# A new list of steps for a sliding-window attention and expert-attention kernel: first unit loaded in row halves, weights in halves, whole-array turns, last stores in four

## The chip, the cores and the metric

The kernel runs on one core of one Trainium2 chip. The metric is the device time of one execution in microseconds (us), as the median of several runs. Its engines are named as in the profile: PE does matmuls (PEld its weight loads), DVE is the vector engine, ACT the scalar engine, POOL the general one, SP the one that issues most loads and stores.

## The reference

Two stages follow each other. The first is attention with a symmetric window of 32 positions, for 8 batches, 8 heads, 576 positions and 64 values per head. The second takes its result as x (576 x 512 per batch) through four attention experts, of which each position uses the two with the largest gate.

```python
# stage 1, q, k, v: (8, 8, 576, 64)
scores = q @ k.T / 8
scores = where(abs(i - j) <= 32, scores, -1e9)
x = softmax(scores) @ v            # -> (8, 576, 512)
# stage 2
logits = x @ w_gate                # 4 experts
w = softmax over the 2 largest logits
for e in range(4):                 # causal attention, width 64
    q, k, v = x @ wq[e], x @ wk[e], x @ wv[e]
    ye = softmax(causal(q @ k.T / 8)) @ v @ wo[e]
    out += (weight of e at each position) * ye
```

## The kernel before, in words

The whole program is one hand-written list, `ORDER`: some 900 short step names, each a function call with its batch and part, the engine behind a colon (v = DVE, a = ACT, g = POOL) and the PSUM banks behind an @. Every engine runs its own steps in the list's order, and waits by semaphores for the data that it needs. A load (`load`, L183) also waits for the last PE instruction that stands before it in the list, so its place in the list sets when SP issues it. Stores wait only for their data, in SP's order.

The steps of one batch b, in the order of the data:

- `lq`, `lk` load four heads of q or k (a unit g = 0 or 1, 0.59 MB); `lv` loads a fifth of v (128 rows of all heads, 256 KB; the last 64 rows, 128 KB). The first two units of batch 0 are loaded in two parts each, of two-row pieces, with four DMAs to a part, some on ACT's queue (form t); all others in one DMA of 18 rows per partition (form e). NAT holds three units of q and three of k.
- `tq`, `tk` turn a unit on DVE (L292 for whole units, L296 for the pieces). `vc` copies v's halves side by side.
- `sc` computes a half of a unit's scores in float32 (80 matmuls), `ex` takes exponentials on ACT (L337), `mk` multiplies by the window's mask on POOL (L341).
- `av` multiplies with v for one of five row groups (32 matmuls), `un` divides by the sums on DVE, `xt`/`xf`/`xb` turn the result and copy it to float32 and bfloat16.
- `ga`, `gt`, `ge`, `gm`, `gu` compute the gate. `pp`/`pe` project q and k for a pair of experts, `pv`/`ve` v.
- `ps`/`xe`/`se` compute causal scores, exponentials (ACT) and the causal cut (POOL), `po`/`oe` the products with v, weighted by the gate.
- `pt`/`ot` turn these (five turns of up to 128 columns), `py` multiplies by wo, `ye` copies the result to one of three Y buffers (one for each w = 0, 1, 2), `st` stores it. w = 0 and 1 are 256 rows each (512 KB), w = 2 the last 64 rows.

The weights wq, wk and wv are loaded whole in `lw0`, `lw1`, `lw2`, through the Y buffers, and cast by `cw0`, `cw1`, `cw2`; wo by `lw3` and `cw3`. Batches overlap: while stage 2 of one batch runs, stage 1 of the next ones does.

## Time and profile before

| what | value |
|---|---|
| median of 3 runs | 270.59 us (270.17 to 270.87) |
| profiled execution | 272.21 us, span 270.5 us |
| PE busy | 224.7 us, 83% of the span |
| DVE, POOL, ACT busy | 172.4, 156.1, 153.1 us |
| DMA moved | 40.66 MB, mean 150 GB/s |

The span goes from the first to the last instruction of the profiled execution. In an order of time, the bracket behind a row is the idle time of the engine just before it, and what ended that; "issue" stands where the profile shows nothing that the engine waited for.

### The profile page before, as it was taken

The numbers are of one execution on the slowest core, as the hardware profiler recorded it, in microseconds if no ns is written. First come the engines' busy times: TensorE is split into PE (matmuls) and PEld (weight loads), VectorE is DVE, ScalarE is ACT, GpSimd is POOL, SyncE is SP. The second block draws the span as 40 slices with busy tenths as digits, with TensorE's granted clock in tenths as the row PEclk, the third lists the DMA queues.
The fourth block names the chain that finished last, engine by engine and source line by source line (L and its number), as shares of the span: only waits on it lengthen the run. The fifth ranks groups of instructions, "written<-read, shape, count | busy, mean of one in ns | idle before, by whom it ended". The sixth has DMA issues, their size and how long they took to land.

```text
span 270.5 us, 12380 instructions
## 1 busy us (share of the span) xinstructions
PE 224.7 (83%) x5526; PEld 180.3 (67%) x5536; DVE 172.4 (64%) x353; ACT 153.1 (57%) x241; POOL 156.1 (58%) x192
## 2 busy tenths in 40 slices
PE   0464468998996999988796999969999899999980
PEld 0443457877886887857675688857787768866640
DVE  0658533865872898577687168568856668675770
ACT  0232233885573696666662469627787655776721
POOL 5048742998596659647968816258929883211400
PEclk9999997999997999999999799979999999999996
DMA  7899693695699697426488243602230042202565
GB/s 159 197 273 243 104 257 99 140 295 182 133 269 237 151 288 213 141 58 159 130 238 288 47 99 74 154 2 95 97 110 12 6 155 82 99 21 80 182 244 198
DMA packets 59350, 40.66 MB, mean 150 GB/s; under 512 B 45728, under 2 KB 51360, under 8 KB 59296
## 3 DMA queue, kind: packets, MB, share of 16 engines
q1 hardware_dynamic: 56736, 38.68, 52.1%
q10 hardware_dynamic: 2560, 1.18, 1.9%
q8 instruction: 43, 0.70, 1.1%
q14 instruction: 11, 0.09, 0.1%
HBM read 30.42 MB, written 9.44 MB: 147 GB/s over the span
## 4 chain that ended last, share of the span: by engine, by line
PE 72%; DMA 11%; issue 8%; DVE 4%; ACT 3%; ACTq 0%; SPq 0%; DVEq 0%
PE PS L177 63%; PE PS L180 9%; DMA qn<-in_q_dram 4%; DMA out_dram<-Y 3%; DMA kn<-in_k_dram 2%; DMA V<-in_v_dram 1%; ACT A L337 1%; DVE Tkn L292 1%; DVE Tqn L292 1%; ACT Y L169 1%; DVE Y L171 0%; ACT VE L169 0%; ACTq L183 0%; ACT WV L169 0%; ACT WK L169 0%
## 5 line engine op out<-in xcount | busy, mean ns | idle before, releaser
L341 POOL TENSOR_TENSOR A<-A,MASKP 128x576 f32<-128x576 f32 x64 | 89.5, 1413 | 37.5 <-ACT A L337 36.9
L177 PE MATMUL PS<-Tqn,Tkn 32*64 32x128 f32 (+3 forms) x2560 | 52.5, 297 | 28.7 <-issue 11.2
L177 PEld LDWEIGHTS PS<-Tqn,Tkn 32*64 32x64 f32 x2560 | 44.9, 148 | 35.7 <-issue 19.1
L337 ACT ACTIVATE A<-PS 128x576 f32<-128x576 f32 x64 | 38.6, 651 | 44.9 <-PE PS L177 44.8
L516 POOL TENSOR_SCALAR_AFFINE_SELECT ATE<-ATE 128x256 bf16<-128x256 bf16 (+1 forms) x80 | 28.9, 383 | 43.1 <-ACT ATE L511 33.5
L511 ACT ACTIVATE ATE<-PS 128x1024 bf16<-128x1024 f32 x48 | 47.6, 1026 | 9.6 <-PE PS L177 9.3
L177 PE MATMUL PS<-V,A 128*64 128x65 f32 (+1 forms) x1280 | 42.1, 227 | 5.2 <-issue 5.1
L177 PEld LDWEIGHTS PS<-V,A 128*64 128x64 f32 (+1 forms) x1280 | 38.1, 136 | 9.2 <-issue 6.7
L292 DVE STREAM_TRANSPOSE Tkn<-kn 128x576 f32<-128x576 f32 x28 | 32.6, 1243 | 5.1 <-PE PS L177 3.2
L292 DVE STREAM_TRANSPOSE Tqn<-qn 128x576 f32<-128x576 f32 x28 | 32.2, 1242 | 3.0 <-PE PS L177 1.9
L171 POOL CAST XTB<-XTF 128x1024 bf16<-128x1024 f32 (+1 forms) x18 | 12.5, 706 | 18.5 <-DVE XTF L171 6.9
L369 DVE TENSOR_TENSOR XN<-PS,RC 128x512 f32<-128x512 f32 x32 | 22.1, 692 | 1.3 <-DVE RC L368 0.2
L169 ACT COPY XTF<-PS 128x128 f32<-128x128 f32 (+1 forms) x23 | 13.4, 632 | 16.4 <-PE PS L180 13.3
L368 DVE RECIPROCAL RC<-PS 128x8 f32<-128x8 f32 x32 | 6.5, 205 | 22.8 <-PE PS L177 22.4
L180 PE MATMUL PS<-ident,XN 128*128 128x128 f32 x144 | 20.9, 294 | 0.0
L171 POOL COPY V<-V 64x2048 f32<-64x2048 f32 (+1 forms) x12 | 20.6, 1717 | 0.4
L169 ACT CAST QKE<-PS 128x576 bf16<-128x576 f32 x23 | 14.4, 642 | 9.3 <-PE PS L177 9.1
L177 PE MATMUL PS<-VE,ATE 128*128 128x65 bf16 x480 | 17.5, 193 | 2.7 <-issue 1.5
L177 PE MATMUL PS<-XTB,WQ 128*128 128x288 bf16 x128 | 19.6, 302 | 0.0
L171 DVE COPY Y<-PS 128x1024 f32<-128x1024 f32 (+1 forms) x12 | 11.5, 956 | 12.7 <-PE PS L177 10.5
L177 PEld LDWEIGHTS <-ATE 128*128 128x128 bf16 x480 | 16.2, 97 | 4.9 <-issue 4.0
L177 PE MATMUL PS<-WO,OTT 128*128 128x512 bf16 (+1 forms) x86 | 18.4, 344 | 1.0 <-DVE OTT L171 0.3
(70 smaller groups left out, 285.0 us busy)
## 6 DMA issues: line engine op xcount, KB each, us to landing
V<-in_v_dram SPq DMA_DIRECT2D x32, 256.0 KB, 4.0
out_dram<-Y SPq DMA_DIRECT2D x16, 512.0 KB, 3.3
kn<-in_k_dram SPq DMA_DIRECT2D x14, 576.0 KB, 5.5
qn<-in_q_dram SPq DMA_DIRECT2D x14, 576.0 KB, 5.4
V<-in_v_dram SPq DMA_DIRECT2D x8, 128.0 KB, 4.3
out_dram<-Y SPq DMA_DIRECT2D x16, 64.0 KB, 2.8
Y<-in_moe_wq_dram SPq DMA_DIRECT2D x1, 512.0 KB, 7.5
Y<-in_moe_wk_dram SPq DMA_DIRECT2D x1, 512.0 KB, 4.0
```

The lines of the kernel that those rows point to most:

```text
L169: nc.scalar.copy(o, i)
L171: eng(c).tensor_copy(o, i)
L177: last_pe[0] = nc.tensor.matmul(*a, **kw)
L180: last_pe[0] = nc.tensor.transpose(*a)
L292: nc.vector.transpose(T[:, :].rearrange("q (p o) -> q o p", o=18)[:, o0:o1], n_[:, o0:o1, 32 * dh:32 * dh + 32])
L337: nc.scalar.activation(AT[(2 * b + g) % NAT_][half][p], two(b0)[:, :, 0:HS], EXP, scale=scale_att)
L341: eng(c).tensor_tensor(out=ap, in0=ap, in1=MASK[:, None, HS * half:HS * half + HS].to_broadcast([128, 2, HS]), op=MULT)
L368: nc.vector.reciprocal(rc, u[:, :, :, 64])
L369: nc.vector.tensor_tensor(out=XN[T // 2][:, T % 2, :].rearrange("p (g h d) -> p g h d", g=2, h=4), in0=u[:, :, :, 0:64], in1=rc[:, :, :, N ...
L511: nc.scalar.activation(chunk(A, ch), two(b0), EXP, scale=scale_moe)
L516: nc.gpsimd.affine_select(ap, ap, pattern=[[0, n], [1, w]], compare_op=IS_GE, fill=0.0, base=0, channel_multiplier=-1)
```

## The change

`ORDER` is written anew as a whole: nearly every step has another place, often another engine for its copies and other banks. In the new list:

- The first unit (batch 0, g = 1; now ahead of g = 0) is loaded and turned in two halves of 9 rows per partition (288 KB in one DMA each); one of the four goes on ACT's queue (form f). g = 0 is loaded whole.
- wq and wk are loaded and cast in halves of two experts (`lw`, `cw` with two numbers), the gate's weights in a step of their own (`lwg`).
- Five steps `zz` are new: each has four matmuls of a zeroed tile, 128 x 128 by 128 x 512, into a bank that nobody reads. `s_zero` zeroes the tile.
- `pt` turns 128 columns in all five turns.
- For batch 7, w = 0 and 1 are computed, copied and stored in two halves each (`py`, `ye`, `st` with a third number): four stores of 256 KB instead of two of 512.

```diff
 ORDER = """
-    lk011:t lq002 s_ones lq011 lq001:t lk001 tq011:v tq002:v tk011:v tq001:v tk001:v lk012:t lv00 lk002 s_warm tk012:v
-    tk002:v s_pads lk100:e sc010@02 lq012:t lv03 lq100:e lv02 sc000@46 ex0000@4 ex0100@0 ex0101@2 s_mask lv01 sc001@40
-    lq110:e lk110:e tk100:e lv04 tq012:v ex0001@6 lw0 sc011@26 ex0010@4 ex0011@0 tq100:e sc100@04 lw1 lk200:e lw2
...
-    oe61@2 ps710@4 xe712@6 xe701@0 py51@6 st42 xe710@4 se713 se710 se701 se703 se700 py50@0 pt60@2 pt61@3 st40 ps711@4
-    ye51:a@6 ye50:v@0 xe711@4 po70@6 ot60:v@2 py52@2 ot61:v@3 ye52:v@2 py61@0 oe70@6 st51 se712 se711 po71@4 oe71@4
-    py60@2 py62@6 pt70@7 st50 pt71@4 ot70:v@7 ot71:v@4 ye61:a@0 ye60:a@2 st52 st61 st60 ye62:v@6 py71@0 ye71:v@0
-    py70@2 py72@4 st62 ye70:a@2 ye72:v@4 st71 st70 st72
+    lq011:f lq012:e lk011:e lk012:e s_warm tq011:e tq012:e tk011:e lq000:e s_ones lk000:e s_zero tk012:e tq000:e
+    lq100:e sc011@02 lk100:e lv03 tk000:e s_pads sc010@46 ex0111@2 lv01 lv00 ex0100@4 zz0@2 s_mask zz3@2 ex0101@6
+    sc000@24 s_ident ex0110@0 mk0111:g ex0001@4 lv02 lwg sc001@06 tq100:e tk100:e mk0101:g mk0110:g zz1@4 ex0011@6
+    ex0000@2 zz2@4 lk110:e lw10 lv12 lv04 mk0001:g mk0100:g mk0011:g ex0010@0 tk110:e vc00:a sc100@46 sc101@02 lq110:e
+    lw00 ex1000@4 vc01:g ex1001@6 mk0000:g av00@4 ex1010@0 un00@4 av01@6 lv11 mk0010:g av02@0 mk1001:g un01@6 un02@0
+    av03@4 ex1011@2 lw11 mk1011:g cw10:g av04@0 lk200:e un03@4 un04@0 lq200:e xt00@2 tq110:e xf00:a@2 xt02@0 xt01@4
+    sc111@62 xf02:a@0 mk1010:g xf01:a@4 xb01:g xb02:g lv10 tk200:e xb00:a cw00:a ex1110@6 sc110@04 ex1101@4 cw11:g
+    lv13 ex1111@2 pp000@6 pp001@4 lw01 pe000:a@6 mk1101:g mk1111:g mk1000:g pe001:v@4 ex1100@0 pp011@2 tq200:e lv14
+    ps001@6 lw2 xe001@6 ps002@0 ga0@4 xe002@0 sc200@60 pe011:a@2 lq210:e cw01:a pp010@2 gt0@4 ge0@4 vc11:g gm0@4
...
+    ps710@2 xe701@4 xe700@6 se711 se700 pt60@1 se713 ge7@0 se701 se712 xe710@2 se710 gm7@0 py50@4 pv70@6 ot60:a@1
+    ve70:a@6 gu7@0 py61@2 py62@0 ye62:a@0 ye61:a@2 ye50:v@4 po70@4 oe70@4 po71@6 oe71@6 py60@0 pt70@2 ot70:v@2 pt71@3
+    ot71:v@3 py72@2 st50 py710@3 st62 py711@4 st61 ye72:v@2 ye60:a@0 st60 ye710:a@3 st72 ye711:v@4 py701@2 st710 st711
+    py700@3 ye701:a@2 st701 ye700:a@3 st700
 """
...
+    ZERO = sb.tile([128, 512], BF16, name="ZERO")
...
+    def s_zero():
+        nc.vector.memset(ZERO, 0.0)
+
+    def zz(c, n, b0):
+        for _ in range(4):
+            mm(PS[:, b0, :], ZERO[:, 0:128], ZERO, start=True, stop=True)
...
-    def lw0():
+    def lwg():
         load(WG[:, :, 0:4], moe_w_gate.rearrange("(t p) e -> p t e", p=128))
-        load(WST[0].rearrange("p (e t d) -> p e t d", e=4, t=4), moe_wq.rearrange("e (t p) d -> p e t d", p=128))
...
+    def lw(n, j):
+        load(WST[n][:, 512 * j:512 * j + 512].rearrange("p (e t d) -> p e t d", e=2, t=4),
+             (moe_wq, moe_wk)[n][2 * j:2 * j + 2].rearrange("e (t p) d -> p e t d", p=128))
...
         for t in range(NQT):
-            w = 128 if t < 4 else 64
-            turn_pe(o[:, 128 * t:128 * t + w], O[0:w, t, :, :].rearrange("p e d -> p (e d)"), ident_bf[0:w, 0:w])
+            turn_pe(o[:, 128 * t:128 * t + 128], O[:, t, :, :].rearrange("p e d -> p (e d)"), ident_bf)
...
+        elif len(at) == 2:
+            copy(c, ysb(b, w)[:, at[0], :], one(at[1]))
...
+        elif at:
+            r = 256 * w + 128 * at[0]
+            nc.sync.dma_start(out[b, r:r + 128, :], ysb(b, w)[:, at[0], :])
```

## The prediction

> **What bounds the kernel now.** I read the page's first lines first, then the stretches, then TensorE's own order of time.

> ```profile
> span 270.5 us, 12380 instructions
> ...
> PE 224.7 (83%) x5526; PEld 180.3 (67%) x5536; DVE 172.4 (64%) x353; ACT 153.1 (57%) x241; POOL 156.1 (58%) x192
> ...
> q8 instruction: 43, 0.70, 1.1%
> ```

> PE is the bound: 224.7 us of 270.5, and no other engine is over 64%. The instruction queue q8 brought 0.70 MB in 43 packets, about 16 KB each. PE and PEld together have 11,062 instructions, which over 43 packets is 257 each: one packet is 128 matmuls with their weight loads.

> ```profile
> 0.00:10.40 10.40, 0.03 (x4) 0.03 (x4) 2.26 (x8) 1.43 (x2) 3.81 (x12) 1.00 0.74 175
> 10.40:47.00 36.60, 23.42 (x668) 20.48 (x676) 19.76 (x49) 11.06 (x16) 17.30 (x17) 0.95 0.83 196
> 47.00:150.00 103.00, 92.38 (x2675) 76.43 (x2674) 74.35 (x140) 66.95 (x111) 78.47 (x79) 0.98 0.71 192
> 150.00:252.60 102.60, 98.89 (x2080) 77.77 (x2086) 67.73 (x143) 67.74 (x109) 53.98 (x79) 0.97 0.26 77
> 252.60:270.50 17.90, 9.95 (x116) 5.58 (x117) 8.31 (x16) 5.96 (x7) 2.50 (x7) 0.85 0.61 219
> ```

> Columns: stretch, length, busy PE, PEld, DVE, ACT, POOL, granted clock, DMA share, GB/s. PE's 45.8 idle us are 10.4 before the first matmul, 13.2 by 47 us, 10.6 by 150, 3.7 by 252.6, and 8.0 in the tail. DMA is at 0.83 just where PE idles most; 175 GB/s x 10.4 us and 196 x 36.6 make 9.0 MB by 47 us.

> What stops PE between 10 and 47 us is in its order of time (bracket: idle time before, and what ended it):

> ```profile
> 10.38 4.33 PE L177 MATMUL PS<-Tqn,Tkn 32*64 32x96 f32 x160 [10.38 <-DVE Tkn L296]
> 15.88 2.40 PE L177 MATMUL PS<-Tqn,Tkn 32*64 32x64 f32 x63 [1.17 <-ACT A L337]
> 19.12 0.81 PE L177 MATMUL PS<-Tqn,Tkn 32*64 32x96 f32 x17 [0.84 <-issue]
> 23.64 3.33 PE L177 MATMUL PS<-Tqn,Tkn 32*64 32x64 f32 x110 [3.70 <-DVE Tqn L296]
> 30.42 3.24 PE L177 MATMUL PS<-Tqn,Tkn 32*64 32x160 f32 x128 [3.46 <-issue]
> 34.15 0.32 PE L177 MATMUL PS<-Tqn,Tkn 32*64 32x96 f32 x2 [0.49 <-issue]
> 34.40 3.95 PE L177 MATMUL PS<-V,A 128*64 128x65 f32 x124
> 41.75 1.39 PE L177 MATMUL PS<-V,A 128*32 128x65 f32 x36 [3.40 <-issue]
> ...
> 46.86 1.35 PE L177 MATMUL PS<-Tqn,Tkn 32*64 32x96 f32 x79
> ```

> Add the counts between stops marked "issue": 160+63 = 223, 17+110 = 127, 128, 2+124 = 126. PE halts every 128 matmuls, waiting for no engine: it waits for its next packet. So the time from one such place to the next is the larger of the 128 matmuls' work and a **turnaround**: 30.42-19.12 = 11.3 us, 34.15-30.42 = 3.7, 41.75-34.15 = 7.6. The queue that issues the loads says why they differ:

> ```profile
> 24.11 0.51 SPq L183 DMA_DIRECT2D Y<-in_moe_wq_dram  x1
> 32.06 0.37 SPq L183 DMA_DIRECT2D Y<-in_moe_wk_dram  x1
> 32.47 1.27 SPq L183 DMA_DIRECT2D kn<-in_k_dram  x1
> 33.79 0.43 SPq L183 DMA_DIRECT2D Y<-in_moe_wv_dram  x1
> 34.32 4.41 SPq L183 DMA_DIRECT2D qn<-in_q_dram  x1
> ```

> Nothing was issued from 24.6 to 32.06, and the turnaround from 30.42 was the shortest, 3.7; four loads were issued in the 2.3 us around 34.15, and it was 7.6. [...]

> **The change, part by part.** Estimates from rows, against this execution (272.21 us for its 270.5 span, 1.7 around it).

> *First unit in halves.* Before, the first scores need four-row pieces, many DMAs each; after, four 288 KB halves, issued at once on two queues.

> ```profile
> L341 POOL TENSOR_TENSOR A<-A,MASKP 128x576 f32<-128x576 f32 x64 | 89.5, 1413 | 37.5 <-ACT A L337 36.9
> ...
> L292 DVE STREAM_TRANSPOSE Tkn<-kn 128x576 f32<-128x576 f32 x28 | 32.6, 1243 | 5.1 <-PE PS L177 3.2
> ...
> V<-in_v_dram SPq DMA_DIRECT2D x32, 256.0 KB, 4.0
> ...
> kn<-in_k_dram SPq DMA_DIRECT2D x14, 576.0 KB, 5.5
> ```

> 288 KB lies between 4.0 and 5.5 us to landing. Issued at about 0.8, the first half is there at 4.8; then VectorE has eight half transposes, as much as four whole ones: 4 x 1.243 = 5.0 us, with two small memsets about 10.2. That is the old 10.38: no gain at the first matmul (9.8 to 12). But now both halves of this unit are there, where the old list ran out and waited 3.70 us at 23.64 for its second q half.

> From 10.2: two scores steps (160 matmuls, 4.33 us) to 14.5; meanwhile four whole transposes for the other unit, 5.0, to 15.2. The new zz steps (16 of the 20 dummy matmuls lie here) fill that gap: 8 x 0.21 = 1.7 us, from the 128x512 group below, to 16.3. The first packet is asked for at about the 96th matmul (224 less 128), at 12.8; before, the same place came at 12.6 (10.38 + 96 x 0.027) and PE went on at 19.12, so 19.3 here, with the queue as full. Scores sc000's rest and sc001 (2.8) and two more zz (1.7) bring 23.8; tq100/tk100 are done by 15.2 + about 2 of pad memsets + 5.0 = 22.3. The next place is just behind, 24.5 by a turnaround of 5.2 (3.7 to 7.6: 23.0 to 26.9). Then comes the one block that is all scores, 2.2 us of work (128/160 x 2 x 1.35); four loads are issued just ahead of it, turnaround 5 (3.7 to 7.6): 29.5. POOL's eight masks at 1.413 and a V copy behind the exponentials end at about 28 to 29, beside it. The old list had these 480 matmuls done at 34.40: -4.9. Then 160 av matmuls at 3.95/124, 5.1 us: 34.6; transposes to 37; lq110, listed after sc101, lands 5.5 after 29.5 and turns in 2.5: 37.5. The next scores start at 38.0 where they started at 46.86: **-8.9**. Ends: by then 8.4 MB must have come (units of 0.59 MB, V pieces of 0.26, weight halves of 0.26); at 196 GB/s that is 43, so -4; without any stop in the all-scores block, -11.

> *Weights in halves.* 0.26 MB pieces that stand in different blocks. But lw01, lv14 and lw2, 0.9 MB, stand in the last 1.3 us ahead of one place (behind sc110 and three pp's), with 3.9 us of work behind it: turnaround 6 to 7.6, and pp010 needs lw01 (4.0 us to landing and a cast): **+2.5** (0 to +5).

> *The later blocks.* I cut both lists into 128s and summed each block's work from 1.35 per scores step, 0.97 per av, 0.97 per pp, 1.0 per po and so on. The old list has four whole blocks of little but scores, 2.1 us each, at the places that stopped PE most; of the later stops these are the largest:

> ```profile
> 81.49 2.11 issue
> ...
> 145.51 2.49 issue
> ```

> All "issue" pieces of 0.4 us or more on the chain from 60 us on make 10.35 us. The new list has no block of 2.1 after the first units; its shortest are 3.05 and 3.2, the others 3.65 to 10. With 3.7 quiet, 4.5 to 5 where loads stand in the last 3 us ahead of the place (nine of them, among them sc500, sc510 and sc601), I get 1.0+0.5+0.3+0.8+0.4+1.8+0.6+0.5+0.6 = 6.5: **-3.9** (from -8 to +1; a load issued just ahead of a place may also come too late to disturb its packet).

> *zz and whole-array turns.* The fifth zz (zz4) lies in busy work: four matmuls of 128x512.

> ```profile
> L177 PE MATMUL PS<-WO,OTT 128*128 128x512 bf16 (+1 forms) x86 | 18.4, 344 | 1.0 <-DVE OTT L171 0.3
> ```

> 18.4/86 = 0.21 each, **+0.9** (0 to +1.7). The other sixteen cost nothing while transposes are late; without that cover, 3.4. They may also speed what follows: scores took 4.33 per 160 at 10.38 and 2 x 1.35 at 46.86, with the granted clock near 1.0 throughout. [...] Turning 128 columns for 64 in the fifth turn: 16 turns, under 0.03 us each, nothing.

> *The end.*

> ```profile
> 255.41 4.93 DMA out_dram<-Y
> ...
> 260.44 1.02 ACT Y L169
> ...
> 262.47 3.21 DMA out_dram<-Y
> ...
> 265.81 0.42 DVE Y L171
> ```

> Three Y buffers: st50's landing (4.93) frees one for ye60, st60's (about as st62's 3.21) frees it for ye70, and what follows st62 ended last. From st50's issue at 255.41 to the end are 15.1 us. After the change the same chain starts at py50 with as much PE work behind it (8.8 for 8.5 us, by the sums): 4.93, 1.02, about 3.3, then two half copies of 0.5 and a last store of about 3.6 with its issue (256 KB instead of the 128 KB with which the old list ends): 13.9. st62 is ahead of st61 and st60, off the end. **-1.2** (-2 to +1.5).

> Sum: -8.9 + 2.5 - 3.9 + 0.9 - 1.2 = **-10.6**. 272.21 becomes 261.6 in a profiled execution; against the median of 270.59, **260.0**. VectorE, ACT and POOL keep their work within some 4 us (ACT has 4 more by its copies), at 57 to 64%.

> **The rivals.** *Stops stay.* The later stops are no smaller, be it that loads meet other packets or that they are no fetches: then -3.9 goes and about 1 of the start: 265.0. For it: most loads still stand within 5 us of some place. Against: the 2.1 us blocks are gone, and 128 is exact.

> *Hardly any stops.* Every load is placed so that its data come behind the packet: then the start has -11, the late stops -8, the weights 0: 270.6 - 11 - 8 + 0.9 - 1.2 = 251.3. For it: the quiet 3.7 lies below nearly all new blocks. Against: 1.2 MB of loads ahead of the all-scores block.

> *Slower: the loads.* The same bytes are wanted 8.9 us earlier, on DMAs at 0.83 already. If fuller queues make the mean turnaround of the first 16 blocks exceed their 4.2 us of work by 1.66, that is 5.9 us, their stops (26.6) eat the old stops of 17.7 and the gain of 8.9; at 6.2 it is +5, 275.5. For it: 7.6 and 11.3 occurred. Against: 3.7 after quiet us, and the block that stopped at 81.49 turned round in about 4.7 (2.11 of stop and by the count 2.6 of work) with loads about.

> **How the numbers follow.** What can be told from no change is 0.3%, 0.8 us. Forecast 0.58 (260.0, its own range 255.5 to 264); stops stay 0.13 (265.0); hardly any stops 0.10 (251.3); slower 0.15 (275.5); the gains just cancel 0.04 (270.6). Faster is 0.58 + 0.13 + 0.10 = 0.81, same 0.04, slower 0.15. The range takes in the forecast, the stops that stay, and a part of the better case: 252 to 268.

> **What would show it.** In the new trace PE should still halt only at matmuls 224, 352, 480 and every 128 on; the old 23.64 wait for a q half should be gone; the first scores start at 10 +- 1, the scores of b1's second unit near 38; "issue" waits of PE in the list of waits should fall from 18.7 to 10 or 12, with none over 3 after 50 us; from st50's issue to the end it should be 13 to 14.5 us. I am wrong if PE's waits for "issue" grow, if VectorE's transposes wait for kn or qn for many us after 20 us, or if the first matmul comes after 12.

## The result, and the profile after

The changed kernel takes 242.29 us (median of 4 runs, 241.64 to 242.96), the one before 270.38: a ratio of 0.897 (0.892 to 0.901). The forecast was 260.0 with a range of 252 to 268. Its sign was right, the size was not: the gain is 28.1 us where 10.6 were expected. Intervals of ratios leave out runs more than 1.5% above the fastest of the same kernel; medians take in all runs.

The page of the changed kernel, its first lines and its granted clock:

```profile
span 240.7 us, 12380 instructions
...
PE 214.6 (89%) x5542; PEld 172.7 (72%) x5556; DVE 170.4 (71%) x351; ACT 155.1 (64%) x241; POOL 157.4 (65%) x193
...
PEclk9999999999999999999999999999999999999997
```

The span fell by 29.8 us. PE's idle time, span less busy, fell from 45.8 to 26.1, by 19.7; its busy time fell by 10.1, though it has 20 more matmuls. So a third of the gain is PE working faster. The same clock row of the kernel before shows one part of where that comes from, and I had not read it:

```profile
PEclk9999997999997999999999799979999999999996
```

Each slice is 6.8 us; the four slices with a 7 each hold a stretch at half clock. Windows on these, of the kernel before (the last columns are clock, DMA share, GB/s):

```profile
43.40:46.70 3.30, 3.30 (x18) 3.16 (x15) 1.18 (x3) 1.80 (x2) 1.05 (x3) 0.50 0.00 0
84.40:87.60 3.20, 3.20 (x63) 3.20 (x62) 0.90 (x2) 1.66 (x4) 1.77 (x2) 0.50 0.88 159
149.20:152.50 3.30, 3.30 (x16) 2.09 (x14) 0.00 (x0) 1.71 (x3) 2.63 (x4) 0.50 0.11 27
179.90:183.20 3.30, 3.30 (x112) 2.68 (x98) 1.35 (x3) 1.42 (x3) 0.42 (x2) 0.50 0.02 5
```

They follow the long halts: 3.40 us to 41.75, 2.11 to 83.6, 2.49 to 148.0, and 2.1 us of idle time (1.51 to 177.99, 0.55 to 179.07) in a chain of other engines that ran from 174.8 to 179.0. In the trace each of the four is one entry of 3.41 us at a granted clock of 0.50, which starts 0.7 to 1.6 us after the idle time ended. Such a halt can be paid twice, once as idle time and once as up to 1.7 us (half of 3.4) lost to half-speed work behind it. Not every halt of this length is: the changed kernel has one of 2.22 us and no such stretch between 15 us and the tail.

The other part is the start, and there the clock row is blind: the first entry of the clock in the trace stands at 33.1 us in the kernel before and at 15.3 in the changed one, and time without an entry counts as full. The orders of time show it. In the kernel before, 160 scores at 10.38 took 4.33 us and 110 at 23.64 took 3.33 (27 and 30 ns each), but 79 at 46.86 took 1.35 (17 ns). In the changed kernel the first 160 took 4.49 us and the second 2.51 (below). For the first 480 scores PE was busy 14.4 us before and 10.1 after, so some 4 us of the gain are a slow start that ended earlier. That it was the clock is argued from these rates: in a run below (the old list with dummies ahead) the granted clock from 10.4 to 47 us was 0.77 on the mean, and 160 scores at 10.71 took 3.87 us, where 160 at 43.20 took 2.71. The start's 4 us and the four stretches (up to 6.8) are more than the 10.1; on the other side stand 4.4 us of dummies in the rows below, so some 3 us less of busy time are left that no run here separates.

PE's order of time at the start, changed kernel:

```profile
9.16 4.49 PE L179 MATMUL PS<-Tqn,Tkn 32*64 32x64 f32 x160 [9.16 <-DVE Tkn L294]
13.58 0.61 PE L179 MATMUL PS<-ZERO 128*128 128x512 bf16 x1
14.40 1.92 PE L179 MATMUL PS<-ZERO 128*128 128x512 bf16 x6 [0.22 <-issue]
16.25 2.51 PE L179 MATMUL PS<-Tqn,Tkn 32*64 32x96 f32 x160
18.70 1.90 PE L179 MATMUL PS<-ZERO 128*128 128x512 bf16 x7
22.06 0.53 PE L179 MATMUL PS<-Tqn,Tkn 32*64 32x96 f32 x16 [1.46 <-DVE Tkn L294]
23.14 2.02 PE L179 MATMUL PS<-Tqn,Tkn 32*64 32x96 f32 x127 [0.55 <-DVE Tkn L294]
27.37 0.50 PE L179 MATMUL PS<-Tqn,Tkn 32*64 32x96 f32 x17 [2.22 <-issue]
27.80 3.96 PE L179 MATMUL PS<-V,A 128*64 128x65 f32 x128
31.93 0.67 PE L179 MATMUL PS<-V,A 128*32 128x65 f32 x32 [0.17 <-DVE XN L371]
32.53 2.19 PE L182 MATMUL PS<-ident,XN 128*128 128x128 f32 x18
34.65 0.55 PE L179 MATMUL PS<-Tqn,Tkn 32*64 32x64 f32 x16
```

The halt of 2.22 us at 27.37 stands at the end of the prediction's all-scores block (behind 479 matmuls by these rows; the prediction counts 480). At matmul 224, inside the second 160 scores (16.25), there is none; 3.70 us for a late q half are gone too. The second unit's scores start at 34.65, in place of 46.86 before: 12.2 us earlier. PE's waits for "issue" in the list of waits of the changed kernel:

```profile
PE PS L179 <- issue: 4.8, 5, 2.2
```

They were 18.7 us in 14 waits.

That these halts are late instruction packets can be read in the trace's DMA records, which hold the packets of queue q8 with their times. Each of the 13 halts of 0.4 us or more in the kernel before ended 1.25 to 1.70 us after such a packet had landed, and the four of over 0.5 us in the changed one 1.28 to 1.53 us after. The place where a packet is asked for is counted as in the prediction, from matmul 96 on every 128; it is an estimate from the first halt at matmul 224, as the trace has only the packet's start. Ahead of the halt that ended at 30.42 the packet started 8.3 us after that place, ahead of 41.75 it was 4.6, ahead of 148.0 it was 4.2; the median is 0.8. After 60 us, 7 of 35 packets of the kernel before started more than 1.5 us late, at most 4.2; in the changed one it was 4 of 33, at most 2.6. So the new list covers the packets with work, and they also come earlier.

### The profile page after: what moved, and what is told of

Read it like the earlier page. It is cut to its first block, busy times and chain, and to the rows that moved or that the text cites. A ratio compares the mean times of both kernels' runs of the same rounds, so it can differ in the third digit from the quotient of the medians.

```text
span 240.7 us, 12380 instructions
## 1 busy us (share of the span) xinstructions
PE 214.6 (89%) x5542; PEld 172.7 (72%) x5556; DVE 170.4 (71%) x351; ACT 155.1 (64%) x241; POOL 157.4 (65%) x193
## 3 DMA queue, kind: packets, MB, share of 16 engines
HBM read 30.42 MB, written 9.44 MB: 166 GB/s over the span
## 4 chain that ended last, share of the span: by engine, by line
PE 81%; DVE 8%; DMA 4%; issue 3%; ACT 2%; ACTq 0%; DVEq 0%
PE PS L179 72%; PE PS L182 8%; DMA kn<-in_k_dram 3%; DVE Tkn L294 3%; DVE Tqn L294 2%; DMA qn<-in_q_dram 2%; ACT ATE L513 1%; DVE OE L553 1%; DVE XN L371 1%; DVE PS L551 0%; DVE RC L370 0%; DVE QKE L173 0%; ACT Y L171 0%; DVE RG L552 0%; ACTq L638 0%
## 5 line engine op out<-in xcount | busy, mean ns | idle before, releaser
L343 POOL TENSOR_TENSOR A<-A,MASKP 128x576 f32<-128x576 f32 x64 | 89.3, 1411 | 24.4 <-ACT A L339 23.8
L179 PE MATMUL PS<-Tqn,Tkn 32*64 32x128 f32 (+3 forms) x2560 | 46.9, 277 | 16.0 <-DVE Tkn L294 11.2
L179 PEld LDWEIGHTS PS<-Tqn,Tkn 32*64 32x64 f32 x2560 | 40.7, 135 | 22.6 <-DVE Tkn L294 12.2
L294 DVE STREAM_TRANSPOSE Tkn<-kn 128x576 f32<-128x576 f32 (+1 forms) x34 | 37.3, 1176 | 8.5 <-DMA kn<-in_k_dram 6.8
L294 DVE STREAM_TRANSPOSE Tqn<-qn 128x576 f32<-128x576 f32 (+1 forms) x34 | 37.2, 1176 | 7.0 <-DMA qn<-in_q_dram 4.6
L179 PE MATMUL PS<-V,A 128*64 128x65 f32 (+1 forms) x1280 | 38.5, 222 | 0.6 <-ACT V L171 0.4
L171 ACT COPY XTF<-PS 128x1024 f32<-128x1024 f32 (+1 forms) x23 | 14.9, 699 | 6.9 <-PE PS L182 6.7
L182 PE MATMUL PS<-ident,XN 128*128 128x128 f32 x144 | 19.3, 277 | 0.0
L179 PE MATMUL PS<-WV,XTB 128*128 128x256 bf16 (+1 forms) x192 | 18.6, 256 | 0.2 <-ACT ATE L513 0.2
L171 ACT CAST QKE<-PS 128x576 bf16<-128x576 f32 x21 | 13.4, 643 | 7.5 <-PE PS L179 7.5
L179 PE MATMUL PS<-XTB,WK 128*128 128x288 bf16 x128 | 18.0, 286 | 0.1
L179 PE MATMUL PS<-QKE 64*128 64x64 bf16 (+4 forms) x192 | 17.0, 278 | 1.1 <-DVE QKE L173 1.1
L171 ACT COPY Y<-PS 128x1024 f32<-128x1024 f32 (+2 forms) x16 | 12.2, 778 | 8.8 <-PE PS L179 8.8
## 6 DMA issues: line engine op xcount, KB each, us to landing
qn<-in_q_dram SPq DMA_DIRECT2D x15, 576.0 KB, 4.7
kn<-in_k_dram SPq DMA_DIRECT2D x15, 576.0 KB, 4.9
V<-in_v_dram SPq DMA_DIRECT2D x32, 256.0 KB, 4.3
out_dram<-Y SPq DMA_DIRECT2D x4, 256.0 KB, 2.5
```

The costliest lines, as they stand in the source:

```text
L171: nc.scalar.copy(o, i)
L179: last_pe[0] = nc.tensor.matmul(*a, **kw)
L182: last_pe[0] = nc.tensor.transpose(*a)
L294: nc.vector.transpose(T[:, :].rearrange("q (p o) -> q o p", o=18)[:, o0:o1], n_[:, o0:o1, 32 * dh:32 * dh + 32])
L343: eng(c).tensor_tensor(out=ap, in0=ap, in1=MASK[:, None, HS * half:HS * half + HS].to_broadcast([128, 2, HS]), op=MULT)
```

## Experiments

In each diff the lines that are not shown are those of the kernel named. Times are medians. The versions were run in four sets, each with the kernel before beside them; its medians were 268.7 to 269.4, some 0.5% below the 270.38 above, so versions are compared within a set where it matters.

### Do the places of the packets decide?

64, 128, 32 and 96 matmuls of one column were put ahead of everything, with PE's places all moved along:

```diff
...
+    def shift():
...
+        for _ in range(64):
+            nc.tensor.matmul(PS[0:32, 7, 0:1], SH[:, 0:32], SH[:, 0:1], start=True, stop=True)
...
     with tc.manual_schedule():
+        shift()
```

Half a packet:

> The changed kernel with 64 tiny matmuls (one column) ahead of everything on PE, in PE's idle time before its data: every place where a packet of 128 matmuls ends moves by half a packet, nothing else moves. Theory A (the new list gains because its work and loads stand right to those places): stops return, PE's issue waits rise from 4.8 us to 10 or more, time 246 to 252. Rival B (the new order is better whatever the places): within 1 us of 242.3.

Measured: 252.1 us, ratio to before 0.946 (0.937 to 0.954). The control:

> Control: 128 tiny matmuls, a whole packet, so all places fall between the same steps as in the changed kernel. Both theories: 242.3 within 1 us, if the tiny matmuls are done before the first data at 9 us; up to +1.5 if not.

Measured: 242.31 us, 0.908 (0.900 to 0.916). A quarter:

> A quarter packet. Theory A: 244 to 250. Rival B: within 1 us of 242.3.

Measured: 254.8 us, 0.947 (0.934 to 0.960). Three quarters:

> The changed kernel with its packet places moved by three quarters of a packet. Theory A: 246 to 256, as with a quarter and a half. Rival: within 1 us of 242.3, the first two shifts having met a bad spot.

Measured: 246.7 us, 0.923 (0.913 to 0.932).

With a quarter the loss was larger than the 244 to 250 of theory A. The list of waits and the clock rows, first with a quarter:

```profile
PE PS L179 <- issue: 15.6, 11, 3.6
```

```profile
PEclk9997979799999999999999999999999999999996
```

Then with half:

```profile
PE PS L179 <- issue: 12.9, 12, 2.9
```

```profile
PEclk9999999999779999999999999999999999999998
```

and the control, a whole packet:

```profile
PE PS L179 <- issue: 4.3, 5, 2.5
```

```profile
PEclk9999889999999999999999999999999999999999
```

Nothing but the places moved, and 4 to 12.5 us came back as halts and half-clock stretches; with a whole packet the time was as before the shift. (The control's two 8s lie between 24 and 36 us: its clock from 10.4 to 47 us was 0.95 on the mean, which is some 3.7 us at half, and its longest halt was 2.5 us. The changed kernel's longest, 2.22 us to 27.37, brought none.) Theory A holds, B falls. The halts stand where the places now are. Counted by weight loads, the tiny matmuls' included, those of over 1 us stand behind 352, 606, 862 and 1498 with a quarter (and one late, behind 4687), and behind 607, 862, 1498, 3156 and 3411 with half: the same counts, though other steps stand there. The largest with half, in PE's order of time:

```profile
66.41 0.69 PE L179 MATMUL PS<-Tqn,Tkn 32*64 32x128 f32 x10 [2.93 <-issue]
```

The old list, moved by half a packet in the same way:

> The kernel before with its packet places moved by half a packet (64 tiny matmuls in PE's idle start). Theory A: its stops move and change size, time 264 to 276, not within 1 us. Rival B: within 1 us of 270.4.

Measured: 265.7 us against 268.9 in its set, ratio 1.005 (0.999 to 1.011). Not told apart from no change, so the expectation of theory A failed for this one. Halts of 15.6 us in 11 waits were left, so the old list was about as badly placed either way.

### What is the load traffic worth?

```diff
-            load(t[:, o0:o1, :]...
+            n = 128 if 2 * b + g < 3 else 1
+            load(t[0:n, o0:o1, :]...
...
+        n = n if b < 2 else 1
         load(t[0:n, 2 * m if m < 4 else 7, :, 0:64], ...
```

> The kernel before, with loads of q, k, v from batch 1's second unit (q, k) and batch 2 (v) on cut to one row: the data of those batches are wrong, the instructions and their places the same, hardly any load traffic. Theory A (loads in flight make the packets late): stops after 60 us fall to the quiet turnaround of 3.7, so only blocks of 2.1 us still stop, by 1.5; and no half-clock stretches: time 252 to 258. Rival B: 268 to 271.

> The same cut in the changed kernel. Theory A: it has little left to gain, 239 to 241. Rival B: the two gain alike.

Measured: 252.3 us (0.941, 0.932 to 0.951) and 237.3 us (0.886, 0.878 to 0.894). The old kernel loses 16 to 18 us to traffic of later batches, the new one 5. The first is in theory A's range, the second below its 239 to 241. So 11 to 13 of the 28.1 us go with the load traffic of later batches: late packets and the slow clock behind them. The old kernel's waits for "issue" fell from 18.7 us to

```profile
PE PS L177 <- issue: 5.3, 5, 1.6
```

with none over 1.6 us, where the longest had been 3.5. But the two kernels without that traffic are still 15 us apart. Where, the stretches show (idle time is length less PE busy, the first pair; the last stretch ends with the span). The kernel before:

```profile
0.00:47.00 47.00, 23.45 (x668) 20.51 (x676) 22.01 (x56) 12.49 (x17) 21.12 (x29) 0.96 0.81 192
47.00:150.00 103.00, 92.38 (x2675) 76.43 (x2674) 74.35 (x140) 66.95 (x111) 78.47 (x79) 0.98 0.71 192
150.00:224.00 74.00, 70.61 (x1622) 55.80 (x1626) 48.26 (x95) 48.14 (x76) 47.60 (x62) 0.96 0.28 80
```

The changed kernel:

```profile
0.00:47.00 47.00, 31.36 (x984) 24.69 (x986) 31.21 (x65) 21.17 (x33) 32.52 (x38) 1.00 0.81 212
47.00:150.00 103.00, 99.48 (x2821) 82.79 (x2825) 81.92 (x160) 71.04 (x115) 78.66 (x86) 1.00 0.68 196
150.00:224.00 74.00, 73.63 (x1623) 58.87 (x1627) 49.98 (x106) 55.40 (x85) 43.72 (x65) 1.00 0.31 95
```

The kernel before with light loads:

```profile
0.00:47.00 47.00, 27.36 (x884) 23.43 (x884) 27.78 (x70) 18.09 (x28) 27.47 (x35) 1.00 0.76 162
47.00:150.00 103.00, 101.25 (x2951) 84.23 (x2949) 80.94 (x148) 75.78 (x124) 83.72 (x89) 1.00 0.08 23
150.00:224.00 74.00, 69.75 (x1485) 55.16 (x1483) 49.92 (x114) 47.92 (x78) 41.05 (x60) 1.00 0.14 50
```

The changed kernel with light loads:

```profile
0.00:47.00 47.00, 32.76 (x1034) 26.10 (x1036) 32.23 (x68) 22.25 (x34) 33.33 (x39) 1.00 0.62 163
47.00:150.00 103.00, 102.69 (x2885) 86.10 (x2882) 84.24 (x163) 75.22 (x120) 81.03 (x90) 1.00 0.09 28
150.00:224.00 74.00, 73.95 (x1620) 58.32 (x1618) 50.01 (x115) 54.87 (x84) 42.98 (x65) 1.00 0.21 73
```

Light loads take the old kernel's idle time between 47 and 150 us from 10.6 to 1.8, and its clock from 0.98 to 1.00, while its idle time from 150 to 224 stays (3.4 and 4.3). There PE waits for other engines, as the chain that ended last has it in the kernel before:

```profile
174.84 1.02 ACT VE L169
...
176.77 2.26 DVE Tkn L292 x2
```

From 174.8 to 179.0 a copy, gate steps and a transpose ran one after another; PE worked on until 176.5 and stood idle for 2.1 us of it, with no packet missing. The new list has 0.4 us idle in that stretch, and 0.05 with light loads. So between the light kernels 5.4 us of idle time lie ahead of 47 us and 5.6 between 47 and 224 (mostly such chains); 1.2 of idle time in the tail and 2.3 of busy time make up the rest of the 14.6 by which the two spans differ.

### What did the old start lose?

```diff
-    lk011:t lq002 s_ones lq011 lq001:t lk001 tq011:v tq002:v tk011:v tq001:v tk001:v lk012:t lv00 lk002 s_warm tk012:v
-    tk002:v s_pads lk100:e sc010@02 lq012:t lv03 ...
+    lk010:f lq010:e s_ones lq000:e lk000:e tk010:e tq010:e tq000:e tk000:e lv00 s_warm
+    s_pads lk100:e sc010@02 lv03 ...
```

(and without tq012:v further on, in the kernel before.)

> The kernel before with its first two units of q and k loaded and turned whole, one DMA each (k's first on ACT's queue), in place of two pieces of four DMAs each; places of packets unmoved. Theory D (the pieces, with many DMAs and the late second q piece, cost the old start): the 3.7 us wait at 23.64 goes, 480 matmuls done 3 to 5 us earlier, time 264 to 268. Rival (the packets after matmul 224 and 352 are the later wait anyway): first matmul about as before, time within 1.5 us of before.

Measured: 264.4 us against 268.7 in its set, 0.987 (0.975 to 0.999). The time and the lost wait are as theory D has them: four whole loads instead of eight pieces of four DMAs each, with the order that this brings, are worth 4 us. The 480 matmuls were done at 32.3, 2.1 us earlier, less than its 3 to 5. The order of time:

```profile
18.23 4.76 PE L177 MATMUL PS<-Tqn,Tkn 32*64 32x64 f32 x160 [0.74 <-ACT A L337]
24.24 4.38 PE L177 MATMUL PS<-Tqn,Tkn 32*64 32x96 f32 x159 [1.26 <-DVE Tqn L292]
31.91 0.42 PE L177 MATMUL PS<-Tqn,Tkn 32*64 32x96 f32 x1 [3.29 <-issue]
```

The 3.70 us wait for the q half is gone, and so are the halts at matmuls 224 and 352, which now lie inside the first and the second row (0.84 and 3.46 us before). A halt of 3.29 us stands at matmul 480, where it was 0.49.

### The named parts, one by one, undone in the changed kernel

First unit whole:

```diff
-    lq011:f lq012:e lk011:e lk012:e s_warm tq011:e tq012:e tk011:e lq000:e ... s_zero tk012:e ...
+    lq010:f lk010:e s_warm tq010:e lq000:e ... s_zero tk010:e ...
```

> The changed kernel with its first unit loaded and turned whole, one DMA for q (on ACT's queue) and one for k: VectorE starts its first turn some 1 us later. Theory A (places of packets and early load order decide, the halves do little): +0.5 to +1.5, so 242.8 to 243.8. Rival (the halves carry the early gain of 11 us): +3 or more.

Measured: 242.42 us. Theory A, at the low end of what it expected: the halves give nothing that can be told; the rival falls.

Weights whole:

```diff
     def lw(n, j):
-        load(WST[n][:, 512 * j:512 * j + 512]..., (moe_wq, moe_wk)[n][2 * j:2 * j + 2]...)
+        if j == 0:
+            load(WST[n]..., (moe_wq, moe_wk)[n]...)
```

> The changed kernel with wk and wq loaded whole at the place of their first half (lw10, lw00), nothing at lw11 and lw01: 0.26 MB more just ahead of the place at matmul 352, and wk whole in time. Theory A (loads near a place cost a stop): +1 to +3. Rival (the halves are worth nothing, the late lw01 ahead of a place goes): 0 to -1.5.

Measured: 241.1 us, ratio 0.902 (0.890 to 0.915). The expected loss did not come; the medians are on the rival's side, the intervals do not part it from the changed kernel.

Last stores whole:

```diff
-    ... py710@3 st62 py711@4 ... ye710:a@3 st72 ye711:v@4 py701@2 st710 st711 py700@3 ye701:a@2 st701 ye700:a@3 st700
+    ... py71@3 st62 ... ye71:v@3 st72 py70@2 st71 ye70:a@2 st70
```

> The changed kernel with the last two results computed, copied and stored whole again (512 KB stores). Prediction's step: +0.5 to +1.5. Rival (the chain of Y buffers decides and the order alone shortened it): 0 within 0.4.

Measured: 241.9 us, 0.896 (0.875 to 0.917). The expected loss did not come: the split stores give nothing.

Dummies of one column:

```diff
-            mm(PS[:, b0, :], ZERO[:, 0:128], ZERO, start=True, stop=True)
+            mm(PS[0:32, b0, 0:1], ZERO[:, 0:32], ZERO[:, 0:1], start=True, stop=True)
```

> The 20 dummy zz matmuls of 512 columns become 20 of one column: same places of the packets, no PE work. Theory C (the dummies end PE's half-speed start early, which the prediction left out): the granted clock stays at half until after 20 us, time +1 to +4. Rival, as predicted: they hide in waits, zz4 costs 0.9: time 0 to -1.5.

Measured: 240.0 us (239.5 to 240.1), where the control with a whole packet had 242.3 in the same set. The same version once more:

> A second look at the changed kernel with one-column dummies: 240 within 0.7, if its gain of 2.3 is real.

Measured: 239.2 us, in one run. Both theories miss: the dummies cost 2.3 us, more than the 0.9 of zz4. The slow start did not last to 20 us as theory C wanted: the second 160 scores took 2.98 us from 13.97 on. But the clock row of the first of the two has half-speed stretches behind it, after a wait of 3.01 us for transposes and a halt of 1.88 us:

```profile
PEclk9997799999999999999999999999999999999998
```

They cost nothing in the end, because PE then waits for transposes and masks anyway; both versions were at the 1024th weight load at 48.6 us. Behind that, halts were 0.8 us in 2 waits for 2.4 in 3, which with the 0.9 of zz4 makes up the gain.

The same question put to the old kernel, 16 dummies and 112 one-column matmuls ahead:

> The kernel before with 16 dummy matmuls of 512 columns and 112 tiny ones ahead (one whole packet, places unmoved): PE is busy from 1 us to about 9. Theory C (a half-speed start costs the old kernel some us up to 33 us): granted clock full from the first scores, 160 scores matmuls in 2.7 us for 4.3, time -1 to -4, less than the matmuls gain because the packet turnaround stays. Rival (clock does not matter): within 1 us of 270.4.

Measured: 264.3 us, 0.979 (0.967 to 0.990). The time fell, by about what theory C expected, but not for its reason: the first 160 scores still took 3.87 us, the clock was 0.77 on the mean from 10.4 to 47 us, and at the 512th matmul only 0.6 us were gained; the rest came from smaller halts later. Inconclusive on the clock.

### Two versions with the costly parts out

> The changed kernel with one-column dummies and whole wk, wq: if both gains add, 238.0 to 239.5; if they are the same stop saved twice, 239.5 to 240.5.

> The same with whole last stores too: within 0.7 of the run with one-column dummies and whole weights.

Measured: 239.7 us, 0.898 (0.888 to 0.907), and 240.7 us, 0.901 (0.891 to 0.909; 0.9 us apart where 0.7 was expected). The first lies where the two gains would be the same stop saved twice. With one-column dummies alone it was 240.0 and, in one run, 239.2, so nothing was added that can be told; by ratios none of these is told apart from the changed kernel.

## Why the prediction was right or wrong

- **What bounds it.** Right: PE, and its halts every 128 matmuls. That the halts go with the places was shown: moved by parts of a packet, the same list loses 4 to 12.5 us; moved by a whole one, nothing. PE's waits for "issue" fell to 4.8 us, further than the 10 or 12 that were named as the sign.
- **First unit.** Forecast: first matmul at 10.2, second unit's scores at 38.0, -8.9. Measured: 9.16 and 34.65, -12.2, just past the better end (-11). The step that was off is the first packet's turnaround, taken over from the old list (6.5 us, resume at 19.3): the packet started 1.1 us after its place instead of 4.1 and landed at 13.66, which makes about 3.5 us, and no halt came there at all. The scores behind it were priced at the slow rate (2.8 us for 104) and ran at the fast one (2.51 for 160). The old list with whole loads had no halt at this place either, nor at matmul 352, where it had been 3.46 us, which points to the old list's many pieces. The cause I gave was wrong too: both halves being there matters, halves as such do not (242.42 whole). The old kernel with whole loads regained 4.2 us by itself.
- **Weights in halves.** Forecast +2.5. Counted by weight loads, the gain did slip from 11.8 at the 768th to 9.1 at the 1024th, and was 11.2 again at the 1152nd: about +1. In the place of the halt stood a wait of 1.05 us for a projection's copy.
- **The later blocks.** This is the step that failed: forecast -3.9, measured about -16 (the gain was 11.2 at the 1152nd weight load and 27.5 at `st50`'s issue, 255.41 before and 227.96 after). Its terms: "issue" pieces of 0.4 us or more on the chain after 60 us fell from 10.35 to 2.4, so -7.9 in place of -3.9. What is left of them in the changed kernel:

```profile
79.77 0.82 issue
...
115.01 0.76 issue
...
147.18 0.84 issue
```

I had let nine places meet a turnaround of 4.5 to 5 where loads stand ahead of them. Measured from the place to the packet's landing and 1.4 us more, two of the 33 after 60 us took so long (5.0 and 4.6), and only three halts were left. The half-clock stretches behind three of the old halts and waits, up to 1.7 each, were not in the sum. And the sum priced only packets: the waits for chains of ACT and DVE, 3 us of idle time from 150 to 224 us, went with the new order too. The three together come to about 16; they were read from the two traces, not undone one by one.

- **zz.** Forecast +0.9; with one column 2.3 less. The cover that I named for sixteen of them was there (the 1024th weight load stands still), the rest is an unpriced change of halts behind.
- **The clock.** The prediction put no term for the clock into its sum. It read the clock off means of long stretches (0.95 to 0.98). The row of slices shows the stretches behind halts, and for the start only the rates of the matmuls show it, since the trace has no entry there; the 4.33 us against 2 x 1.35 that the prediction quotes were the sign. This is the second term that was missing: 10.1 us of busy time, of which light loads alone returned 8.8 in the old kernel. The dummies were not what ended the slow start (2.98 us for the second 160 scores with one-column dummies).
- **The end.** Forecast -1.2, from 15.1 us behind `st50`'s issue to 13.9; measured 12.8, -2.3. But with whole stores it is 12.9, so the order did it.
- **Rivals.** "Hardly any stops" (251.3, chance 0.10) was nearest, and still 9 us too high. "Slower: the loads" did not occur: all halts together were 4.8 us, where it put 26.6 into the first 16 blocks. That the halts are no fetches, one of the two cases of "Stops stay", falls by the times of the packets: 1.25 to 1.70 us from a packet's landing to the end of each of the 13 halts.

## What to carry to other kernels

When one engine stops at a fixed count of its own instructions with nothing to wait for, count them: if the period is fixed, the list of steps and the places of the loads have to be laid around those places, and shifting the places by a few cheap instructions in idle time tests that in one run. Read the clock by slices, not by means, and check it against the time of one matmul: behind three halts of 2.11 to 3.40 us there was a stretch of 3.41 us at a granted clock of 0.50, so a long halt can cost more than its length (up to 1.7 us more, by these numbers). And undo each named part alone: here the first unit's halves, the halves of the weights and the split stores gave nothing that can be told, and the dummies cost 2.3 us. What gave the gain lies in the order of steps and loads; the engines and banks of the copies changed with it and were not tested apart.
